# A block of 256 tokens for the first two slots, and router and remainder work on POOL

## The chip, the cores and the metric

The kernel is one program on one core of a Trainium2 chip. A core has TensorE (PE: matmuls and transposes, with its weight loads as PEld), VectorE (DVE), ScalarE (ACT), GpSimd (POOL) and SyncE (SP, which issues most of the DMA transfers); each works through a queue of its own, and semaphores order the queues against each other. The metric is the time of one execution on the device, in microseconds; less is better.

## The reference, cut to what matters

Three stages follow each other: a retention attention, a dense mixture of experts whose gate is normalised over rows and columns, and a second mixture in which each token goes to one expert. The change lies in the third and in the end of the second.

```python
def _moe2_ref(x, w_gate, w1, w2):            # x: 2304 tokens x 512, 8 experts, hidden size 1024
    logits = x @ w_gate
    expert_idx = np.argmax(logits, axis=1)
    logits_shift = logits - logits.max(-1, keepdims=True)
    probs = np.exp(logits_shift)
    probs /= probs.sum(-1, keepdims=True) + 1e-09
    gate_w = probs[np.arange(N), expert_idx]
    for e in range(E):
        mask = expert_idx == e
        if not mask.any():
            continue
        xe = x[mask]
        h = np.maximum(xe @ w1[e], 0.0)
        out[mask] = gate_w[mask, None] * (h @ w2[e])
```

All is float32. The kernel keeps the precision by splitting each operand into a high part (`hi`, the rounded value) and a remainder (`lo`, what the rounding left), and a product is hi·hi + hi·lo + lo·hi, three matmuls.

## The kernel before

The router finds each token's expert while the dense stage still runs. Tokens of one expert are put into slots of 128 lanes; at least 18 and at most 26 slots hold the 2304 tokens, and 22 are used with these inputs. The first 18 (`NFULL`) are written straight, the others stand behind branches. The router works in two halves: the first half of the tokens (`NEARLY` blocks of 128), whose dense result is done early, gets its ranks during the dense stage, and slots 0 and 1 are filled from it alone; the second half follows once the last dense blocks are done.

The steps of the router (class `Router`) are: `logit_parts` (logits of a block, tile `rpl`, then `L`), `choose` (maximum and one-hot `oh`), `count` (two matmuls `prk` over the one-hots), `totals`, `slots`, `experts` (the list `eidx` of each slot's expert and `echg`, whether the slot's weights differ from those before), `ranks`, `lanes` (the one-hot `Bm` of each token's lane, one operation for each block of 128 tokens), `slots_of`, `onehot` (`r_Z`), `rows` (18 matmuls `pz`, then the token list `gidx` and the scatter list `sidx`), and `gates` with `row_gates` (the gate values of the tokens by an accurate exponential, carried to the slots' rows by 18 matmuls `pzg`). Many of them call DVE through an object `Pumped`, whose line 408 is the line of all operations sent through it: after each it also issues the next operation of a background list, here the gate values.

The third stage is the class `Top1`. For a slot, `gather` fetches its 128 tokens (`xg`, an indirect DMA that POOL issues), `tx` transposes them (`ptx`, then `xth` on ACT and `xtl` on DVE), `load` fetches the expert's weights in eight transfers of 512 KB that SP issues (left out by the hardware condition `echg` where the expert stays), and `split` turns each of the eight pieces `raw` into a high part on ACT (`op0h` to `op6h` and `u7h`) and a remainder on DVE (`op0l` to `op6l`, `u7l`). Pieces 0 to 3 are the first weights, 4 to 7 the second. `hidden` multiplies (two halves of 12 matmuls 128x512, `phs`), `relu` writes `hrow`, `th` transposes it back (`pth`, then `hth` on ACT and the remainder `htl` on DVE) in two halves, and `result` does 24 matmuls 128x512 (`pys`): the first 8 use the high part of the first half of h, the next 4 its remainder, then the second half in the same way. `finish` scales by the gate on ACT and scatters the rows (POOL); `keep` stores an unscaled result in `o` until the gates exist.

While a slot runs, the pieces of the next are split. PE, DVE and ACT issue in the order in which the code is written (`MANUAL`); POOL and SP are ordered by a scheduler. Slots 0 and 1 stand out of line: their steps are written between those of the router, in the last block of the listing.

The remainder is the helper of line 40, one DVE operation with two inputs:

```python
def split_lo(eng, out, src, hi):
    return eng.tensor_tensor(out=out, in0=src, in1=hi.bitcast(F32), op=ALU.subtract)
```

Of the kernel before, what the change touches and what calls it, by code (L numbers as in the profile page):

```python
# [783 lines left out]
class Router:  # L784
# [50 lines left out]
    def choose(self, b, pool):  # L835
# [82 lines left out]
    def gates(self, b, pool):  # L918
# [6 lines left out]
        d = pool.tile([128, n, E], F32, name=f"gd{b}")  # L925
        g = pool.tile([128, n], F32, name=f"g{b}")
# [137 lines left out]
    def experts(self, pool):  # L1064
        v, res = self.v, self.res

        def T(shape, nm):
# [3 lines left out]
        end, cmp, cn = T([E], "end"), T([NSLOT, E], "cmp"), T([NSLOT], "cn")  # L1071
        es, z, ei1 = T([NSLOT], "es"), T([NSLOT], "z"), T([1], "ei1")
        v.tensor_tensor(out=end, in0=self.sta, in1=self.ns, op=ALU.add)
        v.tensor_tensor(
            out=cmp, in0=end.unsqueeze(1).to_broadcast([128, NSLOT, E]),
            in1=t.unsqueeze(2).to_broadcast([128, NSLOT, E]), op=ALU.is_le,
        )
        v.tensor_reduce(out=cn, in_=cmp, axis=AX.X, op=ALU.add)
        v.tensor_scalar(out=cn, in0=cn, scalar1=-1.0, scalar2=None, op0=ALU.add)
        v.scalar_tensor_tensor(  # L1080
            out=es, in0=cn, scalar=self.ei[:, 0:1], in1=cn, op0=ALU.is_ge, op1=ALU.add
        )
        v.tensor_scalar(out=ei1, in0=self.ei, scalar1=1.0, scalar2=None, op0=ALU.add)
        v.tensor_scalar(
            out=z, in0=cn, scalar1=0.0, scalar2=ei1[:, 0:1], op0=ALU.is_lt, op1=ALU.mult
        )
        v.tensor_tensor(out=es, in0=es, in1=z, op=ALU.add)
        v.tensor_scalar(out=es, in0=es, scalar1=float(E - 1), scalar2=None, op0=ALU.min)
        v.tensor_copy(res["eidx"], es)
        v.tensor_tensor(  # L1090
            out=z[:, 1:], in0=es[:, 1:], in1=es[:, 0:NSLOT - 1], op=ALU.not_equal
        )
# [20 lines left out]
    def rows(self, pool):  # L1113
# [43 lines left out]
class Top1:  # L1157
# [194 lines left out]
def build(ctx, tc, q, k, v, moe_w_gate, moe_w1, moe_w2, moe2_w_gate, moe2_w1, moe2_w2,  # L1352
# [136 lines left out]
    with tc.manual_schedule(engines=order):  # L1489
# [65 lines left out]
        }  # L1555
        for n, u in enumerate(range(2 * E - 1, -1, -1)):
# [150 lines left out]
```

## Time and profile before

| | us |
|---|---|
| median of 3 runs | 1976.94 |
| lowest and highest | 1976.7, 1980.82 |
| the profiled execution | 1978.74 |
| its span in the trace | 1977.0 |
| PE busy in the span | 1950.3 |
| DVE busy | 1256.2 |
| ACT busy | 868.3 |
| POOL busy | 180.8 |

The span runs from the first to the last instruction that the trace holds; the execution's own time is 1.7 us longer. The attention ends after some 230 us, the dense stage fills most of the rest, slot 0 begins near 1686 us in the trace and each slot behind the first ones takes about 12 us. A DVE or POOL operation is recorded from its start to its end, and a matmul's record is longer than the distance to the next one, since matmuls are pipelined: for these, the distance is the cost. Under "idle before" stands how long the engine had been idle and what ended that.

### The profile page before, as it was taken

To read this page: it belongs to the slowest core of one execution; us is meant where nothing else is said; L and a number is where in the kernel's file an instruction comes from. 1 tells how busy PE (TensorE), PEld (TensorE's weight loads), DVE (VectorE), ACT (ScalarE), POOL (GpSimd) and SP (SyncE) were. 2 spreads that over 40 slices of the span, in tenths; PEclk is the share of its full clock that TensorE was granted. 3 is DMA by queue.
4 is the path that set the end of the run, shared out by engine and by line. 5 is a ranking of instruction groups with operands and counts; after the bars stand their busy time and mean duration, and the time that the engine had idled before them with its cause. 6 is when DMAs were issued, how large, how long until landed. Compare 5 with 4: busy or idle time off the path is not lost.

```text
span 1977.0 us, 25401 instructions
## 1 busy us (share of the span) xinstructions
PE 1950.3 (99%) x9608; PEld 1626.9 (82%) x9608; DVE 1256.2 (64%) x2089; ACT 868.3 (44%) x1484; POOL 180.8 (9%) x200
## 2 busy tenths in 40 slices
PE   8999999999999999999999999999999999999998
PEld 7877888888888888888888888888888888778886
DVE  7997565555555555555565555665556665889998
ACT  6765424322223333233334333333333334489997
POOL 6662000000000000000010000000000000122211
PEclk9999999999999999999999999999999999999999
DMA  5531111111111011111211211111111213111755
GB/s 130 140 69 65 43 43 43 43 43 43 43 43 36 29 43 43 43 43 43 95 51 43 64 43 43 63 44 43 64 43 43 64 45 126 37 50 44 281 192 220
DMA packets 112111, 134.94 MB, mean 68 GB/s; under 512 B 62190, under 2 KB 62446, under 8 KB 111600
## 3 DMA queue, kind: packets, MB, share of 16 engines
q1 hardware_dynamic: 106960, 121.92, 19.3%
q0 software_dynamic: 3680, 11.02, 1.7%
q8 instruction: 77, 1.26, 0.3%
q10 hardware_dynamic: 1344, 0.33, 0.1%
q14 instruction: 50, 0.41, 0.1%
HBM read 182.53 MB, written 12.58 MB: 99 GB/s over the span
## 4 chain that ended last, share of the span: by engine, by line
PE 77%; issue 9%; DVE 8%; DMA 2%; POOL 2%; ACT 1%; SPq 0%; POOLq 0%; DVEq 0%; ACTq 0%
PE pyt L731 39%; PE pha L609 17%; PE phc L609 9%; PE phr L706 5%; PE phb L609 4%; DMA out_dram<-o,sidx 2%; DVE qbd L40 1%; POOL xg L1186 1%; DVE s L40 1%; POOL out_dram L1344 1%; DVE xa L287 1%; PE rpl L832 1%; DVE Sf L249 1%; DVE vlo L33 1%; DVE kT L33 1%
## 5 line engine op out<-in xcount | busy, mean ns | idle before, releaser
L731 PE MATMUL pyt<-w2hi,hhi 128*128 128x512 f32 x1024 | 402.2, 393 | 0.6 <-DVE xa L742 0.6
L731 PE MATMUL pyt<-w2hi,hlo 128*128 128x512 f32 x1024 | 398.9, 390 | 0.0
L731 PE MATMUL pyt<-w2lo,hhi 128*128 128x512 f32 x1024 | 398.5, 389 | 0.0
L635 ACT ACTIVATE q<-pha 128x512 f32<-128x512 f32 x192 | 114.6, 597 | 271.4 <-PE pha L609 268.9
L623 ACT ACTIVATE hhi<-q 128x512 fp32r<-128x512 f32 x192 | 121.4, 632 | 248.6 <-DVE q L631 248.6
L731 PEld LDWEIGHTS pyt<-w2hi,hlo 128*128 128x128 f32 x1024 | 192.2, 188 | 40.6
L731 PEld LDWEIGHTS pyt<-w2hi,hhi 128*128 128x128 f32 x1024 | 192.3, 188 | 40.3 <-DVE xa L742 1.4
L731 PEld LDWEIGHTS pyt<-w2lo,hhi 128*128 128x128 f32 x1024 | 192.4, 188 | 38.9
L624 DVE SCALAR_TENSOR_TENSOR hlo<-q,hhi 128x512 fp32r<-128x512 f32 x192 | 133.0, 692 | 96.8 <-ACT hhi L623 90.8
L742 DVE SCALAR_TENSOR_TENSOR xa<-pyt,P,xa 128x512 f32<-128x512 f32 x140 | 105.0, 750 | 134.5 <-PE pyt L731 133.7
L631 DVE TENSOR_TENSOR q<-phb,q 128x512 f32<-128x512 f32 x64 | 44.3, 692 | 166.6 <-PE phb L609 166.6
L742 DVE SCALAR_TENSOR_TENSOR xb<-pyt,P,xb 128x512 f32<-128x512 f32 x120 | 90.0, 750 | 90.4 <-PE pyt L731 90.3
L631 DVE TENSOR_TENSOR q<-phc,q 128x512 f32<-128x512 f32 x128 | 87.7, 685 | 34.0 <-PE phc L609 33.1
L561 ACT ACTIVATE w3h<-raw 128x512 fp32r<-128x512 f32 x31 | 19.6, 631 | 159.0 <-DVE raw L567 158.9
L567 DVE TENSOR_TENSOR raw<-raw 128x512 f32<-128x512 f32 x124 | 85.1, 686 | 1.1
L40 DVE TENSOR_TENSOR w2lo<-raw,w2hi 128x512 fp32r<-128x512 f32 x124 | 84.6, 683 | 0.0
L714 DVE SCALAR_TENSOR_TENSOR rlo<-phr,rhi 128x512 fp32r<-128x512 f32 x32 | 22.1, 691 | 87.7 <-ACT rhi L713 87.7
L587 ACT ACTIVATE w2hi<-raw 128x512 fp32r<-128x512 f32 x124 | 77.1, 622 | 0.0
L561 ACT ACTIVATE w4h<-raw 128x512 fp32r<-128x512 f32 x31 | 19.6, 631 | 115.2 <-DVE raw L567 115.2
L40 POOL TENSOR_TENSOR op2l<-xb,op2h 128x1024 fp32r<-128x1024 f32 x1 | 2.4, 2389 | 713.1 <-ACT op2h L494 713.1
L224 POOL TENSOR_SCALAR_AFFINE_SELECT s<-s 128x512 fp32r<-128x512 f32 (+1 forms) x96 | 57.3, 635 | 49.8 <-DVE s L40 49.8
L1186 POOL DMA_INDIRECT xg<-x2d,gidx x24 | 38.1, 1587 | 217.3 <-PE phc L609 100.6
(392 smaller groups left out, 4634.7 us busy)
## 6 DMA issues: line engine op xcount, KB each, us to landing
raw<-in_moe_w_dram SPq DMA_DIRECT2D x180, 512.0 KB
raw<-in_moe_w_dram SPq DMA_DIRECT2D x62, 1024.0 KB
kt<-in_k_dram SPq DMA_DIRECT2D x32, 128.0 KB
vt<-in_v_dram SPq DMA_DIRECT2D x32, 128.0 KB
qt<-in_q_dram SPq DMA_DIRECT2D x32, 128.0 KB
x2d<-xa SPq DMA_DIRECT2D x10, 256.0 KB
xbd<-xb SPq DMA_DIRECT2D x1, 2048.0 KB
xb<-xbd SPq DMA_DIRECT2D x2, 1024.0 KB
```

What stands on the lines that cost most here:

```text
L40: return eng.tensor_tensor(out=out, in0=src, in1=hi.bitcast(F32), op=ALU.subtract)
L567: nc.vector.tensor_tensor(out=q(*out), in0=q(*a), in1=q(*b), op=op)
L587: nc.scalar.activation(hi, self.raw2[:, fc, :], AF.Copy)
L609: self.nc.tensor.matmul(bank, ww[:, k, 128 * p:128 * p + 128], xx[:, k, :], start=start and n == 0, stop=stop and n == 5, skip_group_check ...
L623: nc.scalar.activation(hi, c, AF.Relu)
L624: nc.vector.scalar_tensor_tensor(out=lo, in0=c, scalar=0.0, in1=hi.bitcast(F32), op0=ALU.max, op1=ALU.subtract)
L631: self.nc.vector.tensor_tensor(out=s, in0=p, in1=s, op=ALU.add)
L635: self.nc.scalar.activation(t, c, AF.Copy)
L706: nc.tensor.matmul(pt[:, j, :], w[:, k, 128 * j:128 * j + 128], xr[x][:, xi, k, :], start=n == 0, stop=n == 11,)
L731: nc.tensor.matmul(pt, hh, ww, start=n == 0, stop=n == 11)
L742: nc.vector.scalar_tensor_tensor(out=acc, in0=pt, scalar=P[:, i, e:e + 1], in1=acc, op0=ALU.mult, op1=ALU.add)
L1186: self.nc.gpsimd.indirect_dma_start(out=self.xg[t % 3], out_offset=None, in_=self.x2d[0:rows, :], in_offset=bass.IndirectOffsetOnAxis(ap=i ...
```

## The change

Slots 0 and 1 become one block of 256 tokens. `block_hidden` multiplies with the weights as the stationary operand and both slots' tokens as the moving one, in four quarters of 24 matmuls 128x256 (`phb`), so that h comes out transposed already: its high part (`hb`) is written by ACT and its remainder by DVE, and the transposes `pth` of these slots are gone. The results of the two slots are still 24 matmuls each. For that, both slots' gathers go to the place where slot 0's was, and both `tx` into the last dense unit.

The router's `experts` is rewritten for POOL, where a reduction is a tree of additions and fused operations are split into two; every second `Bm` of the second half goes to POOL; `rows` issues the gathers of slots 2 and 3 right after `gidx`. The remainders of u7 (slot 0), op4 (slot 2), then inside slot 2 of u7, op1, op3 and op5, and inside slot 3 of op1 and op4, go to POOL. The gate values of the first half are issued in the last dense units, in steps between the products; those of the second half inside slot 2, four operations behind each split. Three slots' results are kept unscaled (tiles `o`, now four) and finished in slot 3 instead of two finished in slot 2.

```diff
-            (nc.gpsimd if i % 4 == 3 and b == 0 else v).tensor_scalar(
+            (nc.gpsimd if (i % 2 if b else i % 4 == 3) else v).tensor_scalar(
...
     def experts(self, pool):
-        v, res = self.v, self.res
+        g, res = self.nc.gpsimd, self.res
...
+        g.tensor_tensor(out=end, in0=self.sta, in1=self.ns, op=ALU.add)
+        g.tensor_tensor(
+            out=cmp, in0=t.unsqueeze(2).to_broadcast([128, NSLOT, E]),
+            in1=end.unsqueeze(1).to_broadcast([128, NSLOT, E]), op=ALU.subtract,
+        )
+        g.tensor_scalar(out=cmp, in0=cmp, scalar1=0.0, scalar2=None, op0=ALU.is_ge)
+        for h in (4, 2):
+            g.tensor_tensor(out=cmp[:, :, 0:h], in0=cmp[:, :, 0:h], in1=cmp[:, :, h:2 * h], op=ALU.add)
...
+        g.tensor_tensor(out=cn, in0=cmp[:, :, 0:1], in1=cmp[:, :, 1:2], op=ALU.add)
...
         v.tensor_copy(res["gidx"], tok)
+        then()
...
-    def split(self, c):
+    def split(self, c, pool=False):
         hi, lo = self.unit(c)
         self.nc.scalar.activation(hi, self.raws[c], AF.Copy)
-        split_lo(self.nc.vector, lo, self.raws[c], hi)
+        split_lo(self.nc.gpsimd if pool else self.nc.vector, lo, self.raws[c], hi)
...
+    def block_hidden(self, g, mid=None):
+        ph = self.php.tile([128, 2, 256], F32, name="phb2", tag="ph")
+        for j in range(2):
+            if j and mid:
+                mid()
+            f0 = 256 * g + 128 * j
+            n = 0
+            for k in range(KD):
+                wh, wl = self.unit(k)
+                for w, x in ((wh, 0), (wl, 0), (wh, 1)):
+                    self.nc.tensor.matmul(
+                        ph[:, j, :].rearrange("p (s t) -> p s t", s=2), w[:, f0:f0 + 128],
+                        self.xts[x][:, :, k, :], start=n == 0, stop=n == 11,
+                    )
+                    n += 1
+        hi, lo = (t[:, 2 * g:2 * g + 2, :] for t in self.hb)
+        self.nc.scalar.activation(hi, ph, AF.Relu)
+        self.nc.vector.scalar_tensor_tensor(
+            out=lo, in0=ph, scalar=0.0, in1=hi.bitcast(F32), op0=ALU.max, op1=ALU.subtract
+        )
+    def block(self, s):
+        return tuple(t[:, :, 128 * s:128 * s + 128] for t in self.hb)
...
-    def slot(self, t, mid=None):
+    def slot(self, t, mid=None, pooled=(), tick=lambda: None, kept=False):
+        def split(c):
+            self.split(c, c in pooled)
+            tick()
 
...
-        self.finish(t, py)
+            split(4)
+            split(5)
+        o = self.keep(t, py) if kept else self.finish(t, py)
...
+        gates0 = Pumped(nc.vector)
...
-            D.hidden(u)
+            if n == NEARLY + 4:
+                gates0.bg.append(ro.gates(0))
+            D.hidden(u, (), lambda: gates0.step(2))
...
+                gates0.step(1 if j < 6 else 8)
...
-                t1.gather(0)
+                for t in range(2):
+                    t1.gather(t)
...
+                    if j in (5, 6):
+                        t1.tx(j - 5, aux, "rt")
                     if j < 7:
                         t1.split(j)
-                    if j == 5:
-                        t1.tx(0, aux, "rt")
...
-        t1.gather(1)
-        t1.split(7)
-        ro.v.bg = [ro.gates(0, tmp)]
-        h0, h1 = t1.begin(), t1.begin()
-
-        ph = t1.hidden(0, 0, None, range(0, 2))
-        next(lp)
-        ph = t1.hidden(0, 0, ph, range(2, 4))
+        t1.block_hidden(0, lambda: next(lp))
         drain(lp)
-        t1.relu(0, ph, h0[0])
+        t1.split(7, True)
         ro.choose(1, tmp)
-        ro.v.bg.append(ro.gates(1, tmp))
-        ph = t1.hidden(0, 1, None, range(0, 1))
+        t1.block_hidden(1)
         ro.count(1)
-        t1.hidden(0, 1, ph, range(1, 4))
-        t1.relu(1, ph, h0[0])
         ro.totals(1)
         ro.slots(tmp)
-        t1.th(0, *h0)
-        t1.th(1, *h0)
-        t1.tx(1, t1.ptp, "pt")
-        py = t1.result(*h0[1:])
         ro.experts(tmp)
         t1.ahead(2)
         for c in range(4, 8):
             t1.load(2, c)
-        o0 = t1.keep(0, py)
-
         ro.ranks(1)
+        t1.block_hidden(2)
         ro.lanes(1)
         ro.slots_of(tmp)
-        ph = t1.hidden(1, 0)
-        t1.relu(0, ph, h1[0])
-        ph = t1.hidden(1, 1)
-        t1.relu(1, ph, h1[0])
+        t1.block_hidden(3)
         ro.onehot(tmp)
-        ro.rows(tmp)
-        for t in (2, 3):
-            t1.gather(t)
-        t1.th(0, *h1)
-        t1.th(1, *h1)
+        py = t1.result(*t1.block(0))
+        o0 = t1.keep(0, py)
+        py = t1.php.tile([128, DM], F32, name="pys1", tag="ph")
+        t1.result(*t1.block(1), py, slice(0, 8))
+        ro.rows(tmp, lambda: [t1.gather(t) for t in (2, 3)])
         for c in range(4):
             t1.split(c)
-        py = t1.result(*h1[1:], None, slice(0, 12))
-        t1.split(4)
+        t1.result(*t1.block(1), py, slice(8, 24))
         t1.tx(2, t1.ptp, "pt")
-        t1.result(*h1[1:], py, slice(12, 24))
+        t1.split(4, True)
         t1.split(5)
-        ro.v.rest()
         t1.ahead(3)
         o1 = t1.keep(1, py)
+        bg = Pumped(nc.vector)
+        bg.bg = [ro.gates(1, tmp)]
+        o2 = t1.slot(2, None, (7, 1, 3, 5), lambda: bg.step(4), True)
+        bg.rest()
         rg = ro.row_gates(tmp)
         next(rg)
 
         def mid():
             drain(rg)
-            t1.finish(0, o0, o0)
-            t1.finish(1, o1, o1)
-
-        for t in range(2, NFULL):
-            t1.slot(t, mid if t == 2 else None)
+            for t, o in enumerate((o0, o1, o2)):
+                t1.finish(t, o, o)
+        for t in range(3, NFULL):
+            t1.slot(t, mid if t == 3 else None, (1, 4) if t == 3 else ())
```

On DVE, at the turn to slot 2: before, from the products `r_Z` of the router's one-hots on. `op6l` and `u7l` are remainders of slot 2's own weights, `op0l` and those behind it of slot 3's, `htl` is the remainder of h.

```order
L408 TENSOR_TENSOR r_Z<-r_Z,gparts 128x18x26 x3
L40 TENSOR_TENSOR op6l<-raw_13843,op6h 128x1024
L40 TENSOR_TENSOR u7l<-raw_13844,u7h 128x1024
L40 TENSOR_TENSOR op0l<-raw_101,op0h 128x1024
L40 TENSOR_TENSOR htl<-pth,hth 128x512
L40 TENSOR_TENSOR op1l<-raw_101,op1h 128x1024
L40 TENSOR_TENSOR op2l<-raw_102,op2h 128x1024
L40 TENSOR_TENSOR xtl<-ptx,xth 128x512
L40 TENSOR_TENSOR htl<-pth,hth 128x512
```

The same place now, from the `xtl` of slot 2 to the first `htl`; `gd` and the tiles `g_` are gate values.

```order
L40 TENSOR_TENSOR xtl<-ptx,xth 128x512
L40 TENSOR_TENSOR op5l<-raw_13867,op5h 128x1024
L40 TENSOR_TENSOR op6l<-raw_13868,op6h 128x1024
L946 TENSOR_TENSOR gd_14553<-L_8949,m_14206 128x64
L348 TENSOR_SCALAR g_msk<-gd_14553 128x64
L350 TENSOR_SCALAR g_xc<-gd_14553 128x64
...
L360 TENSOR_SCALAR g_ki<-g_k 128x64
L40 TENSOR_TENSOR op0l<-raw_101,op0h 128x1024
L363 TENSOR_SCALAR g_q<-g_r 128x64
L366 SCALAR_TENSOR_TENSOR g_q<-g_q,g_r 128x64 x3
L40 TENSOR_TENSOR htl<-pth,hth 128x512
```

The products `r_Z` and the remainder of u7 are no longer ahead of the first `htl`; twelve operations of the gate values are, four of them left out above.

On POOL, behind the gathers of slots 0 and 1: before, only gathers and scatters follow.

```order
L913 TENSOR_SCALAR Bm<-c_8941,ro_13022 128x128 x2
L1186 DMA xg_13847<-x2d,gidx_69 128x512
L1186 DMA xg_14104<-x2d,gidx_69 128x512
L1186 DMA xg_14105<-x2d,gidx 128x512
L1186 DMA xg_13847<-x2d,gidx 128x512
```

Now, from the end of the expert list on.

```order
L1121 CAST echg<-r_z 128x25
L1212 DMA xg_14140<-x2d,gidx 128x512
L1212 DMA xg_13872<-x2d,gidx 128x512
L1212 DMA xg_13873<-x2d,gidx 128x512
L1212 DMA xg_14140<-x2d,gidx 128x512
L40 TENSOR_TENSOR op4l<-raw_13866,op4h 128x1024
L40 TENSOR_TENSOR u7l<-raw_13869,u7h 128x1024
L40 TENSOR_TENSOR op1l<-raw_101,op1h 128x1024
L1212 DMA xg_13872<-x2d,gidx 128x512
L40 TENSOR_TENSOR op3l<-raw_102,op3h 128x1024
L40 TENSOR_TENSOR op5l<-raw_13867,op5h 128x1024
```

Ahead of these stand 20 operations of the list with four `Bm` between them, and ahead of those the remainder of u7 for slot 0; all three came from DVE.

## Rows read from the trace of the kernel before

**Rows 1.** The page's first part: busy us of each engine, share of the span, instructions.

```profile
PE 1950.3 (99%) x9608; PEld 1626.9 (82%) x9608; DVE 1256.2 (64%) x2089; ACT 868.3 (44%) x1484; POOL 180.8 (9%) x200
```

**Rows 2.** Windows of slots 2, 3 and 4; columns in the prediction.

```profile
1720.06:1733.49 13.43, 13.30 (x80) 10.80 (x78) 11.49 (x17) 10.05 (x14) 2.79 (x3) 1.00 0.17 51
...
1733.49:1747.20 13.71, 12.60 (x62) 10.03 (x61) 13.06 (x13) 13.04 (x17) 4.71 (x4) 1.00 0.23 78
...
1747.20:1759.55 12.35, 12.35 (x62) 10.12 (x60) 11.21 (x12) 11.15 (x14) 3.01 (x2) 1.00 0.14 43
```

**Rows 3.** Waits of PE from 1677 us on: sum, count, mean.

```profile
PE pth L1265 <- ACT hrow L1258: 1.1, 1, 1.1
...
PE pz L1118 <- DVE r_Z L408: 1.1, 1, 1.1
...
PE prk L859 <- DVE g_k L354: 1.0, 1, 1.0
...
PE ptx L1232 <- DMA xg<-x2d,gidx: 0.9, 1, 0.9
...
PE ptx L1232 <- ACT L L833: 0.3, 1, 0.3
...
PE pys L1283 <- ACT hth L1267: 0.2, 1, 0.2
```

**Rows 4.** Windows behind the wait for g_k; the granted clock stands third from the end.

```profile
1694.00:1696.00 2.00, 2.00 (x7) 1.58 (x6) 2.00 (x17) 0.00 (x0) 0.00 (x0) 0.56 0.00 0
...
1696.00:1698.00 2.00, 2.00 (x8) 1.38 (x7) 1.66 (x13) 0.61 (x2) 0.00 (x0) 0.59 0.00 0
```

**Rows 5.** Timeline of PE, the first of 24 matmuls 128x256 and what follows them.

```profile
237.25 0.28 PE L706 MATMUL phr<-xrh,w0h 128*128 128x256 f32 x1
...
240.12 0.40 PE L609 MATMUL phc<-op3h,w3h 128*128 128x512 f32 x1
```

**Rows 6.** Timeline of PE: 24 hidden matmuls apart, and four transposes.

```profile
1704.35 0.39 PE L1253 MATMUL phs<-op0h,xth 128*128 128x512 f32 x1
...
1709.56 0.39 PE L1253 MATMUL phs<-op3h,xtl 128*128 128x512 f32 x1
...
1751.28 0.60 PE L1265 MATMUL pth<-ident,hrow 128*128 128x128 f32 x4
...
1751.63 0.48 PE L1253 MATMUL phs<-op2h,xth 128*128 128x512 f32 x1
```

**Rows 7.** Timeline of POOL and DVE in the dense stage.

```profile
987.55 2.39 POOL L40 TENSOR_TENSOR op2l<-xb,op2h 128x1024 fp32r<-128x1024 f32 x1 [713.07 <-ACT op2h L494]
...
988.23 0.75 DVE L742 SCALAR_TENSOR_TENSOR xa<-pyt,P,xa 128x512 f32<-128x512 f32 x1 [1.97 <-PE pyt L731]
...
988.90 2.13 DVE L40 TENSOR_TENSOR op0l<-xb,op0h 128x1024 fp32r<-128x1024 f32 x1
...
1002.27 1.21 DVE L40 TENSOR_TENSOR op5l<-xb,op5h 128x1024 fp32r<-128x1024 f32 x1
```

**Rows 8.** Timeline around slot 1's end, several engines.

```profile
1691.77 0.18 ACT L833 ACTIVATE L<-rpl 128x8 f32<-128x8 f32 x1 [1.53 <-PE rpl L832]
...
1712.35 0.18 DVE L408 CAST gidx<-r_tok 128x26 uint32<-128x26 f32 x1
...
1713.45 0.99 POOL L1186 DMA_INDIRECT xg<-x2d,gidx  x1 [55.57 <-ACT hth L1267]
...
1716.85 0.63 PE L1232 MATMUL ptx<-ident,xg 128*128 128x128 f32 x4 [0.87 <-DMA xg<-x2d,gidx]
...
1720.81 0.50 PE L1253 MATMUL phs<-op0h,xtl 128*128 128x512 f32 x1
```

**Rows 9.** Timeline and groups: Bm on both engines, a 512-column remainder on POOL.

```profile
1553.45 1.22 POOL L913 TENSOR_SCALAR Bm<-c,ro 128x128 bf16<-128x128 bf16 x2 [545.27 <-PE pyt L731]
...
1554.03 0.70 DVE L408 TENSOR_SCALAR Bm<-c,ro 128x128 bf16<-128x128 bf16 x3
...
L40 POOL TENSOR_TENSOR klo<-kt,khi 128x512 fp32r<-128x512 f32 x16 | 20.6, 1290 | 9.5 <-DMA gq_sb<-in_c_gq_dram 7.9 <-POOL s L224 1.2 <-ACT khi L149 0.4
```

More of the change, by code (lines that the diff above doesn't have):

```diff
@@ L383, in drain, with __init__, tile @@
             return s.value
+class Slab:
+    def __init__(self, ap):
+        self.ap, self.off, self.tags = ap, 0, {}
+    def tile(self, shape, dt, name, tag):
+        n = shape[1]
+        if tag not in self.tags:
+            self.tags[tag] = self.ap[:, self.off:self.off + n]
+            self.off += n
+        t = self.tags[tag]
+        return t if dt == F32 else t.bitcast(dt)
 class Pumped:
@@ L916, in lanes, with gates @@
             )
-    def gates(self, b, pool):
+    def gates(self, b, pool=None):
         nc, v, r = self.nc, self.nc.vector, self.B[b]
         i0, n = r["i0"], r["n"]
-        d = pool.tile([128, n, E], F32, name=f"gd{b}")
-        g = pool.tile([128, n], F32, name=f"g{b}")
+        if pool is None:
+            d, g = r["eq"], r["mm"]
+            pool = Slab(self.xt.rearrange("p a b -> p (a b)"))
+        else:
+            d = pool.tile([128, n, E], F32, name=f"gd{b}")
+            g = pool.tile([128, n], F32, name=f"g{b}")
         v.tensor_tensor(
@@ L1070, in experts @@
         t = self.c("t")
-        end, cmp, cn = T([E], "end"), T([NSLOT, E], "cmp"), T([NSLOT], "cn")
+        end, cmp, cn = T([E], "end"), T([NSLOT, E], "cmp"), T([NSLOT, 1], "cn")
         es, z, ei1 = T([NSLOT], "es"), T([NSLOT], "z"), T([1], "ei1")
[L1073 to L1076, printed above, removed]
-        )
@@ L1078, in experts @@
[L1078 to L1084, printed above, removed]
+        g.tensor_tensor(out=end, in0=self.sta, in1=self.ns, op=ALU.add)
+        g.tensor_tensor(
+            out=cmp, in0=t.unsqueeze(2).to_broadcast([128, NSLOT, E]),
+            in1=end.unsqueeze(1).to_broadcast([128, NSLOT, E]), op=ALU.subtract,
+        )
@@ new lines, in experts @@
+        g.tensor_scalar(out=cmp, in0=cmp, scalar1=0.0, scalar2=None, op0=ALU.is_ge)
+        for h in (4, 2):
+            g.tensor_tensor(out=cmp[:, :, 0:h], in0=cmp[:, :, 0:h], in1=cmp[:, :, h:2 * h], op=ALU.add)
+        g.tensor_tensor(out=cn, in0=cmp[:, :, 0:1], in1=cmp[:, :, 1:2], op=ALU.add)
+        cn = cn.rearrange("p s a -> p (s a)")
+        g.tensor_scalar(out=cn, in0=cn, scalar1=-1.0, scalar2=None, op0=ALU.add)
+        g.tensor_scalar(out=es, in0=cn, scalar1=self.ei[:, 0:1], scalar2=None, op0=ALU.is_ge)
@@ L1085, in experts @@
+        g.tensor_tensor(out=es, in0=es, in1=cn, op=ALU.add)
+        g.tensor_scalar(out=ei1, in0=self.ei, scalar1=1.0, scalar2=None, op0=ALU.add)
+        g.tensor_scalar(
             out=z, in0=cn, scalar1=0.0, scalar2=ei1[:, 0:1], op0=ALU.is_lt, op1=ALU.mult
         )
[L1087 to L1091, printed above, removed]
-        )
@@ L1094, in experts @@
-        v.scalar_tensor_tensor(
-            out=res["echg"][:, 1:], in0=t[:, 1:], scalar=self.inc[:, E - 1:E], in1=z[:, 1:],
-            op0=ALU.is_lt, op1=ALU.mult,
-        )
-        v.tensor_copy(res["nslot"], self.inc[:, E - 1:E])
+        g.tensor_tensor(out=es, in0=es, in1=z, op=ALU.add)
+        g.tensor_scalar(out=es, in0=es, scalar1=float(E - 1), scalar2=None, op0=ALU.min)
+        g.tensor_copy(res["eidx"], es)
+        g.tensor_tensor(out=z[:, 1:], in0=es[:, 1:], in1=es[:, 0:NSLOT - 1], op=ALU.subtract)
@@ L1100, in onehot @@
+        g.tensor_scalar(
+            out=z[:, 1:], in0=z[:, 1:], scalar1=0.0, scalar2=0.5, op0=ALU.is_equal, op1=ALU.is_lt
+        )
+        g.tensor_scalar(
+            out=cn, in0=t, scalar1=self.inc[:, E - 1:E], scalar2=None, op0=ALU.is_lt
+        )
+        g.tensor_tensor(out=z[:, 1:], in0=z[:, 1:], in1=cn[:, 1:], op=ALU.mult)
+        g.tensor_copy(res["echg"][:, 1:], z[:, 1:])
+        g.tensor_copy(res["nslot"], self.inc[:, E - 1:E])
     def onehot(self, pool):
@@ L1111, in onehot, with rows @@
         v.tensor_tensor(out=Z[:, :, 2, :], in0=A1, in1=bc(self.c("i")), op=ALU.mult)
-    def rows(self, pool):
+    def rows(self, pool, then):
         nc, v, res, Z = self.nc, self.v, self.res, self.Z
@@ L1168, in __init__ @@
         self.xts = [pool.tile([128, 2, KD, 128], F32R, name=f"xt{x}") for x in "hl"]
-        self.xg = [pool.tile([128, DM], F32, name="xg0")]
+        self.xg = [pool.tile([128, DM], F32, name=f"xg{i}") for i in range(2)]
         self.regs = {}
@@ L1308, in slot @@
         if nxt:
-            self.split(1)
+            split(1)
         self.relu(1, ph, h)
         if nxt:
-            self.split(2)
+            split(2)
             self.tx(t + 1, self.ptp, "pt")
```

17 lines of the change are left out of this document (9 added, 8 removed).

## The prediction

> **What bounds the kernel now.** I read the busy line first: TensorE (PE) works 1950.3 us of a span of 1977.0 [rows 1], so time can come only from where PE idles, runs slowly or does work that can go. The windows of slots 2, 3 and 4 come next [rows 2]; their columns after the sum are PE, PEld, DVE, ACT, POOL, granted clock, DMA share and GB/s. In slot 4 PE is busy all 12.35 us, and so it is in the slots behind it; slot 2 takes 13.43 and slot 3 takes 13.71. The slots of one stream follow each other on PE, so whatever moves the start of slot 5 moves the end by as much. Then the waits of PE over the last 300 us [rows 3]: hrow (ScalarE, ACT) 1.1, r_Z 1.1, g_k 1.0, the gather xg 0.9, and 0.2 to 0.3 each for L and hth. All lie before 1721 us but part of the first, which stands for one instruction in slot 3. A third view shows a loss that is no wait: between 1694 and 1698 the granted clock is 0.56 and 0.59 [rows 4], that is 1.2 GHz for most of it, right after PE's wait for g_k; I put the loss at 1.9 us (4 us at 0.575 do the work of 2.3, which loses 1.7; the fall begins and ends a little outside).
>
> **The change part by part.** I walked the engines' queues of the changed program in order with the durations of the rows, and compare the start of the third hidden matmul of slot 2 (1720.81 before [rows 8]), of slot 3 (1733.49 [rows 2]) and of slot 5 (1759.55).
>
> *The block.* The 72 matmuls of 256 columns that follow the router's last logits cost 2.87/24 = 0.1197 each [rows 5], 8.62 us; they replace 36 of 512 columns at 5.21/23 = 0.2267 (the 24 from the first to the second of [rows 6]), 8.16 us: +0.5. Four transposes cost 1751.63 - 1751.28 = 0.35 [rows 6]. Sixteen pth transposes go, and four ptx move ahead of the logits: 5 x 0.35 = -1.8. The waits for hrow and r_Z and the small ones for L and hth go: 1.1 + 1.1 + 0.3 + 0.2 = -2.7. The wait for g_k (VectorE, DVE) stays about 1.1: the ranks need oh, and oh stands behind u7's remainder. Before, that remainder was in DVE's queue; now it is on POOL, starts after u7h, which starts after the last L (1691.77 [rows 8]) and takes 1.05 of ACT, and runs to about 1695.9, while the block's second quarter covers PE to 1694.9 only. I take the 1.9 of the low clock as gone, since the matmuls around it are shorter and the wait is as long; if it stays, the result is 1.9 higher. New are three waits in front of slot 2. gidx comes at 1710.7 instead of 1712.5; from there to ptx took 4.3 [rows 8], and 16 result matmuls (3.6) follow it on PE, so ptx waits 1.5 instead of 0.9. Then xth: 1.1. Then xtl: 1.5, for it stands in DVE behind op0l to op3l (4 x 1.14), and op0 must land first, which the router's list now on POOL decides (end about 1709.7, plus a load that I estimate at 2.0 from the 2.4 between the end of the gather's issue and ptx [rows 8]). Together 0.5 - 1.8 - 2.7 - 1.9 + 0.6 + 1.1 + 1.5 + 0.1 = -2.6, and 0.2 to 0.3 comes back in the last dense unit, where ptx of slot 1 now stands: **-2.4** at the third hidden matmul.
>
> *Slot 2.* This is what decides. POOL gets the remainders of op4, u7, op1, op3 and op5, DVE the second half's gate values, four operations behind each remainder. What POOL costs is shown in the dense stage [rows 7]: op2l on POOL takes 2.39, from 987.55 to 989.94. DVE's op0l beside it was due at 988.90 and is recorded with 2.13, which is the 1.04 until POOL ended and then its own 1.09; undisturbed such an operation takes 1.21. In the same stretch xa, which reads PSUM, runs in its usual 0.75 beside POOL's op2l. A second pair 10 us later shows the same. So a DVE operation with both inputs in SBUF stands still while POOL's runs. In slot 2 the queue of DVE from xtl to the remainder htl of the first half of h is op5l, op6l, 12 gate operations, op0l: 3 x 1.14 = 3.4, the gate operations 0.2 each as the small row of gidx [rows 8], 2.5, and htl 0.6. Into it fall four POOL operations, op4l, u7l, op1l and op3l, 4 x 2.39 = 9.6, of which 0.7 is past when it begins: 15.4 in all. PE in that time has 22 hidden matmuls, 8 transposes of th and tx, 8 result matmuls and four transposes more, 30 x 0.227 + 3 x 0.35 = 7.9, and then the ninth result matmul wants htl: a wait of 7.3. The second half's htl comes 1.3 late in the same way (op5l on POOL). Without waits slot 2 from its third matmul is 11.9; with them 20.3, against 12.7 before: **+7.7**.
>
> *Slots 3 and 4.* The row gates (three products over 18x26, the sums, the gate itself) and three scalings of o, which cost slots 2 and 3 together 1.1 + 1.4 us above slot 4 before [rows 2], now fall into slot 3 alone, and op1l and op4l on POOL hold DVE for another 4.8. DVE's slack is what a slot leaves it, 12.35 - 11.21 = 1.1 [rows 2], in each. I get 29.2 instead of 26.1 for the two: **+3.2**. (The POOL work takes two remainders, 2.3, from DVE in exchange; that is in the sum.)
>
> *What costs nothing.* The first half's gate values run beside the last dense matmuls, where DVE is 64% busy over the span [rows 1]; two o more are kept by ACT, which has slack (11.15 of 12.35 with its waits [rows 2]). If this cover were gone, 33 operations of 0.2 would cost up to 6.6, but nothing on PE waits for them there. The gather of slot 1 goes to the dense stage with slot 0's (0.99 of POOL [rows 8], which is 9% busy over the span); three scatters of o go a slot later, and only o's buffers, now four, wait for them. One bound is wide: POOL's some 20 small operations for the expert list are not in the trace before. Its nearest rows are Bm at 0.61 [rows 9] and the 512-column remainder at 1.29, against 2.39 for 1024: 0.19 plus 2.15 ns per column. By that line the list ends as above. If each costs 0.1 to 0.2 more, op0 lands 2 to 4 us later and PE waits 2.3 to 4.5 more; if the list were free, at most the 1.5 of xtl would go.
>
> The Bm rows [rows 9] are weak evidence on another point: three DVE Bm, each with one SBUF input, take 0.70 in all while POOL does two at 0.61, so they are not held whole. The Trainium skill (SBUF — State Buffer, section Who interferes with whom) says that an operation with two SBUF inputs contends with GpSimd's reads, that copies, casts and tensor_scalar can take the shared ports as well, and that the loser of the pair is blocked for the whole instruction. By the row the single-input gate operations run free, and the sum is +8.5; by the rule in full they would be held too, and it would be +9.6.
>
> **The sum** is -2.4 + 7.7 + 3.2 = +8.5 against the profiled execution (1978.74 us), 1987.2 there. That execution stands 1.8 above the median, 1976.94, so on the median I forecast 1985.5.
>
> **The rivals.**
> *A, the slots don't feel POOL.* If DVE and POOL run side by side in the slots, the walk gives -2.4 for the block, slot 2 is near even, and DVE has gained seven remainders: together -4.4, or 1972.5. For it: the 0.70 of the three Bm; nothing stops DVE between two POOL operations. Against it: the pair of [rows 7] and the one behind it, which are the same operation at the same size.
> *B, near even.* The holding is as shown but POOL falls behind: its remainders start later than I let them, when DVE has passed htl, so that two of the four fall behind htl, and htl of the second half is not late: 8.5 - 2 x 2.39 - 1.3 = +2.4, or 1979.3. For it: POOL's queue holds the list, four gathers and the remainders, in one row. Against it: a late remainder delays the matmul that wants it.
> *C, slower still.* The list on POOL sets the start of slot 2 (0.2 per operation more, +4.5), or the wait of 7 us for htl is followed by the low clock as the one before 1694 was [rows 4]: 16 result matmuls at 0.2 more, +3.2. Together 1988.7 to 1993. It decides from the point where op0 lands after 1714.
>
> **How the numbers follow.** The forecast has 0.56 with a range of its own of 1981.5 to 1988.7, from the bounds above (a load's landing at 1 or 3 us is 1 either way, a POOL remainder of 2.0 instead of 2.39 takes 1.6 off, the low clock 1.9 on). A has 0.18, B 0.13, C 0.13. The range of 8 in 10 runs from 1972.5 to 1992: it takes in B, most of C and A down to its own time. About 0.2%, 4 us, is what a measurement of this kernel tells from no change. A lies at that bound and gives 0.12 to faster and 0.06 to no change, B 0.12 to no change and 0.01 to slower: faster 0.12, no change 0.18, slower 0.70.
>
> **What would show it.** Right: in the profile after, DVE's op5l, op6l and op0l in slot 2 are recorded with 2.5 to 3.6 us instead of 1.2, PE waits some 7 us for htl of the first half in slot 2, and slot 3 is over 14 us; the waits for hrow and r_Z are gone, and slot 2 begins 2 to 3 us earlier. Wrong: remainders of 1.2 on DVE beside POOL's 2.39, or PE's first long wait on op0h (then it is the list), or POOL's remainders behind the matmul that wants them.

## The result

The changed kernel takes 1988.97 us (median of 4 runs, 1988.01 to 1992.45) against 1977.38 (4 runs, 1976.7 to 1980.82): a ratio of 1.0059, 95% interval 1.0046 to 1.0071, so 11.6 us slower. The forecast was 1985.5, in a range of 1972.5 to 1992; its own narrower range, 1981.5 to 1988.7, ends 0.3 below the measured time.

The profiled execution took 1992.45 us with a span of 1990.7, 13.7 more than the span of before. Of that, 3.5 us lie in the attention, which the change doesn't touch: the first matmul of [rows 5] stands at 240.73 instead of 237.25. In two of the experiments below, whose attention is the same too, it stands at 236.47 and at 240.53, so I compare stretches and not positions.

| stretch on PE | before | forecast | after |
|---|---|---|---|
| first matmul of [rows 5] to the last logits | 1453.5 | +0.3 | 1454.3 (+0.8) |
| last logits to the third hidden matmul of slot 2 | 30.0 | -2.7 | 25.6 (-4.4) |
| from there to slot 3 | 12.7 | +7.7 | 23.6 (+10.9) |
| slots 3 and 4 | 26.1 | +3.2 | 28.6 (+2.5) |
| sum | | +8.5 | +9.8 |

Behind slot 5 nothing differs: from its start to the last matmul are 209.5 and 209.6. The +0.8 of the first row is not told from scatter: up to the last logits the experiments on the changed kernel have the same code, and their traces show 1453.4 to 1454.7 there.

The remaining 1.8 between 9.8 and the 11.6 of the medians is not in this table; the profiled execution of before stood 1.4 above its own median. The last experiment shows a likely place. Its program is that of before up to slot 2 (but for one more buffer for o), and from the last logits to the third hidden matmul of slot 2 its trace has 28.9 instead of 30.0: there PE's clock doesn't fall behind the wait for g_k. So the 30.0, and the -4.4 worked out from it, hold 1.1 that this stretch does not always cost, and against that trace the block is worth 3.3. That the median run of before also lacks the low clock is not shown.

The first part of the page after (busy us, share, instructions), to be held against [rows 1], and the windows of slots 2, 3 and 4, which answer to [rows 2]:

```profile
PE 1953.9 (98%) x9640; PEld 1631.1 (82%) x9640; DVE 1264.5 (64%) x2064; ACT 866.9 (44%) x1481; POOL 210.5 (11%) x232
```

```profile
1719.91:1744.26 24.35, 15.52 (x61) 11.82 (x62) 22.60 (x31) 12.55 (x16) 15.96 (x8) 0.79 0.13 36
1744.26:1757.29 13.03, 13.03 (x80) 10.88 (x78) 11.16 (x17) 9.44 (x13) 4.61 (x3) 1.00 0.08 21
1757.29:1772.84 15.55, 13.15 (x62) 9.87 (x61) 12.89 (x12) 14.24 (x19) 8.76 (x6) 1.00 0.21 74
```

PE does 3.6 us more and yet fills less of the span; slot 2 is the place, and slot 4 is now longer than slot 3. The waits of PE from 1670 us on in the changed kernel (sum, count, longest), to be held against [rows 3], whose third figure is the longest as well:

```profile
PE pys L1334 <- DVE htl L40: 9.1, 2, 8.8
PE pth L1316 <- ACT hrow L1309: 1.5, 1, 1.5
PE prk L874 <- DVE oh L423: 1.0, 1, 1.0
PE ptx L1258 <- DMA xg<-x2d,gidx: 0.9, 1, 0.9
PE phs L1279 <- ACT xth L1260: 0.7, 1, 0.7
PE phs L1279 <- DVE op3l L40: 0.6, 1, 0.6
```

The wait for r_Z is gone, prk still waits 1.0, and a new wait of 8.8 us for htl is longer than all of [rows 3] together. The wait for hrow is not one of the block: it stands in slot 4 now, and before it stood in slot 3, as PE's timeline of the kernel before has it:

```profile
1738.84 0.66 PE L1265 MATMUL pth<-ident,hrow 128*128 128x128 f32 x4 [1.11 <-ACT hrow L1258]
```

The timeline of DVE in slot 2 (start, us, operation) tells what htl stood behind:

```profile
1719.89 0.69 DVE L40 TENSOR_TENSOR xtl<-ptx,xth 128x512 fp32r<-128x512 f32 x1 [0.16 <-ACT xth L1260]
1721.78 6.01 DVE L40 TENSOR_TENSOR op5l<-raw,op5h 128x1024 fp32r<-128x1024 f32 x1 [1.20 <-ACT op5h L1247]
1727.71 3.40 DVE L40 TENSOR_TENSOR op6l<-raw,op6h 128x1024 fp32r<-128x1024 f32 x1
1731.04 0.21 DVE L946 TENSOR_TENSOR gd<-L,m 128x64 f32<-128x64 f32 x1
1731.28 0.20 DVE L348 TENSOR_SCALAR g_msk<-gd 128x64 f32<-128x64 f32 x1
1731.39 3.05 DVE L350 TENSOR_SCALAR g_xc<-gd 128x64 f32<-128x64 f32 x1
...
1737.46 0.68 DVE L40 TENSOR_TENSOR htl<-pth,hth 128x512 fp32r<-128x512 f32 x1
...
1741.49 0.68 DVE L40 TENSOR_TENSOR htl<-pth,hth 128x512 fp32r<-128x512 f32 x1
1742.09 1.90 DVE L964 CAST gparts<-g 128x8 bf16<-128x8 f32 x1
```

And the timeline of POOL in the same slot:

```profile
1721.93 2.42 POOL L40 TENSOR_TENSOR op4l<-raw,op4h 128x1024 fp32r<-128x1024 f32 x1
1724.30 2.40 POOL L40 TENSOR_TENSOR u7l<-raw,u7h 128x1024 fp32r<-128x1024 f32 x1
1727.07 2.96 POOL L40 TENSOR_TENSOR op1l<-raw,op1h 128x1024 fp32r<-128x1024 f32 x1 [0.38 <-ACT op1h L1247]
...
1732.03 2.35 POOL L40 TENSOR_TENSOR op3l<-raw,op3h 128x1024 fp32r<-128x1024 f32 x1
1741.59 2.38 POOL L40 TENSOR_TENSOR op5l<-raw,op5h 128x1024 fp32r<-128x1024 f32 x1 [7.21 <-ACT op5h L1247]
```

op5l is recorded with 6.01: POOL's op4l and u7l end at 1726.70, and op5l's own 1.09 follows [rows 7]. op6l ends 1.1 behind POOL's op1l (1730.03). g_xc, a TENSOR_SCALAR with one input in SBUF and 0.2 long elsewhere, ends at 1734.44, 0.06 behind op3l; its record begins 0.64 before that of op3l, and what held it in that time is not shown. A CAST takes 1.90 and ends with op5l of POOL. htl reads PSUM: the first one has no operation of POOL beside it, the second (1741.49) runs beside op5l and still takes its usual 0.68. PE, on its timeline, then runs on at half its speed:

```profile
1728.85 0.60 PE L1316 MATMUL pth<-ident,hrow 128*128 128x128 f32 x4
1738.20 1.22 PE L1334 MATMUL pys<-op4h,htl 128*128 128x512 f32 x2 [8.76 <-DVE htl L40]
...
1740.92 0.63 PE L1334 MATMUL pys<-op6h,hth 128*128 128x512 f32 x1
...
1743.06 0.43 PE L1334 MATMUL pys<-u7l,hth 128*128 128x512 f32 x1
...
1744.26 0.39 PE L1279 MATMUL phs<-op0h,xth 128*128 128x512 f32 x1
```

The window of the profile there (PE, PEld, DVE, ACT, POOL, granted clock, DMA share, GB/s) names the cause, 1.2 GHz:

```profile
1740.00:1742.00 2.00, 2.00 (x6) 1.54 (x5) 1.90 (x7) 1.51 (x2) 0.41 (x1) 0.50 0.00 0
...
1743.00:1745.00 2.00, 2.00 (x10) 1.58 (x9) 1.90 (x5) 0.55 (x2) 0.97 (x1) 0.97 0.04 8
```

The first 11 result matmuls behind the wait, 1738.20 to 1743.06, take 4.86 us where 11 at 0.2267 [rows 6] would take 2.49: 2.4 lost. The wait and these are 11.2, which is the 10.9 that slot 2 grew by, within 0.3.

### The profile page after: what moved, and what is told of

The parts are those of the page before. It is cut to its first block, busy times and chain, and to the rows that moved or that the text cites. A ratio compares the mean times of both kernels' runs of the same rounds, so it can differ in the third digit from the quotient of the medians.

```text
span 1990.7 us, 25472 instructions
## 1 busy us (share of the span) xinstructions
PE 1953.9 (98%) x9640; PEld 1631.1 (82%) x9640; DVE 1264.5 (64%) x2064; ACT 866.9 (44%) x1481; POOL 210.5 (11%) x232
## 4 chain that ended last, share of the span: by engine, by line
PE 78%; issue 9%; DVE 7%; DMA 2%; POOL 2%; ACT 1%; SPq 0%; POOLq 0%; ACTq 0%; DVEq 0%
PE pyt L746 39%; PE pha L624 17%; PE phc L624 9%; PE phr L721 5%; PE phb L624 4%; DMA out_dram<-o,sidx 2%; DVE qbd L40 1%; POOL xg L1212 1%; DVE s L40 1%; POOL out_dram L1400 1%; PE po L274 1%; DVE xa L287 1%; PE rpl L847 1%; PE pys L1334 1%; DVE Sf L249 1%
## 5 line engine op out<-in xcount | busy, mean ns | idle before, releaser
L576 ACT ACTIVATE w3h<-raw 128x512 fp32r<-128x512 f32 x31 | 19.6, 631 | 159.6 <-DVE raw L582 159.5
L576 ACT ACTIVATE w4h<-raw 128x512 fp32r<-128x512 f32 x31 | 19.6, 631 | 114.1 <-DVE raw L582 114.1
L928 POOL TENSOR_SCALAR Bm<-c,ro 128x128 bf16<-128x128 bf16 x6 | 4.0, 672 | 545.4 <-PE pyt L746 545.3
```

## The experiments

Each run states its median beside that of the kernel before, timed on the same chip. The last two columns are from one trace of each, in us. An interval behind a ratio is at 95%.

| kernel | us | before | third hidden matmul of slot 2 to slot 3 | slots 3 and 4 |
|---|---|---|---|---|
| before | | 1977.38 | 12.7 | 26.1 |
| changed | 1988.97 | 1977.38 | 23.6 | 28.6 |
| no remainders on POOL in slots 2, 3 | 1980.15 | 1977.26 | 15.2 | 29.0 |
| gate values between the router's operations | 1982.17 | 1977.26 | 17.3 | 28.4 |
| both of these | 1976.34 | 1977.26 | 12.3 | 27.5 |
| list on DVE | 1987.26 | 1977.26 | 21.3 | 28.9 |
| both, u7 on DVE | 1978.76 | 1977.61 | 13.5 | 27.5 |
| both, results finished one by one | 1974.61 | 1977.61 | 12.3 | 25.4 |
| all of these | 1973.46 | 1977.61 | 12.4 | 25.4 |
| POOL remainders in halves | 1988.53 | 1977.61 | 23.6 | 28.6 |
| before, results finished one by one | 1976.90 | 1978.47 | 12.7 | 24.7 |

**No remainders on POOL in the slots.**

```diff
-        t1.split(4, True)
+        t1.split(4)
-        o2 = t1.slot(2, None, (7, 1, 3, 5), lambda: bg.step(4), True)
+        o2 = t1.slot(2, None, (), lambda: bg.step(4), True)
-            t1.slot(t, mid if t == 3 else None, (1, 4) if t == 3 else ())
+            t1.slot(t, mid if t == 3 else None, ())
```

> Theory P (POOL's remainders in slots 2 and 3 hold DVE's operations): all seven remainders go back to DVE, the gate values stay in slot 2. DVE's queue ahead of the first htl of slot 2 is then 5 remainders of 1.14, 12 small ones of 0.21 and 0.6, 8.8 us, no longer than what PE has to do, so the wait of 8.8 us and the low clock behind it go; DVE still has some 17 us of work in slot 2 and gives 3 to 4 us of it to slots 3 and 4. About 1979 us (1975 to 1982). Theory G (the 33 gate operations put into slot 2 are what delays htl, POOL only relieves DVE): DVE gets 8 us more work ahead of and behind htl, so no faster than now, 1987 or more. Theory L (the expert list on POOL sets the start of slot 2): no change beyond 2 us, since the list stays.

1980.15 us, 8.8 less than the changed kernel, although DVE now does seven remainders more. Its operations in slot 2 are back to their own lengths; g_xc stands here for the single-input ones:

```profile
1722.06 1.22 DVE L40 TENSOR_TENSOR op5l<-raw,op5h 128x1024 fp32r<-128x1024 f32 x1
1723.30 1.23 DVE L40 TENSOR_TENSOR op6l<-raw,op6h 128x1024 fp32r<-128x1024 f32 x1
...
1724.81 0.19 DVE L350 TENSOR_SCALAR g_xc<-gd 128x64 f32<-128x64 f32 x1
...
1729.02 0.68 DVE L40 TENSOR_TENSOR htl<-pth,hth 128x512 fp32r<-128x512 f32 x1
```

The longest wait for htl is 2.2 instead of 8.8, and theory G falls: more work on DVE made it faster. L falls too, since the list stayed where it was. But P had the wait go altogether, and slots 3 and 4 still take 29.0.

**Gate values between the router's operations.**

```diff
         ro.choose(1, tmp)
+        ro.v.bg.append(ro.gates(1, tmp))
...
-        bg = Pumped(nc.vector)
-        bg.bg = [ro.gates(1, tmp)]
-        o2 = t1.slot(2, None, (7, 1, 3, 5), lambda: bg.step(4), True)
-        bg.rest()
+        ro.v.rest()
+        o2 = t1.slot(2, None, (7, 1, 3, 5), kept=True)
```

> The gate values of the second half are issued between the router's DVE operations, as before the change; POOL keeps its seven remainders. Theory P: DVE ahead of the first htl still has 3 remainders of 1.14 and stands behind three or four of POOL's 2.39, 11 to 13 us against PE's 8, so a wait of 3 to 5 us stays: about 1984 us (1981 to 1986). Theory G: the wait goes, slots 2 and 3 are no longer than before, and with the block's gain about 1974.

1982.17, where P expected 1981 to 1986. The longest wait for htl is 2.5, a little less than P's 3 to 5. POOL's remainders hold DVE as in the changed kernel, here DVE's remainders alone:

```profile
1721.56 2.83 DVE L40 TENSOR_TENSOR op5l<-raw,op5h 128x1024 fp32r<-128x1024 f32 x1 [1.15 <-ACT op5h L1247]
1724.32 3.42 DVE L40 TENSOR_TENSOR op6l<-raw,op6h 128x1024 fp32r<-128x1024 f32 x1
1727.66 3.40 DVE L40 TENSOR_TENSOR op0l<-raw,op0h 128x1024 fp32r<-128x1024 f32 x1
...
1731.58 3.88 DVE L40 TENSOR_TENSOR op2l<-raw,op2h 128x1024 fp32r<-128x1024 f32 x1
```

Taken one by one, the remainders are worth 8.8 and the gate values 6.8; they share a part, since either shortens the same queue.

**Both.** The two edits above together.

> Both at once: no remainder on POOL in slots 2 and 3, gate values of the second half between the router's operations. Theory P: slots 2 to 4 cost what they did before the change, and the block's gain stays (4.4 us in the traces up to the third hidden matmul of slot 2): about 1973 us (1971.5 to 1975). Theory G: the same as with the gate values moved alone, within 2 us of it. Theory L: 1976 or more.

1976.34, ratio 0.9993 (0.9984 to 1.0003): the slowdown is gone, 12.6 us below the changed kernel, and slot 2 costs 12.3. It is not the 1973 that P expected. Of the difference, 1.4 is in slots 3 and 4, 27.5 against 26.1; most of the rest is again what the stretches of the traces do not hold (here they add up to -2.6, and the medians differ by -0.9). ACT's timeline shows what slots 3 and 4 lose:

```profile
1741.42 0.60 ACT L1318 ACTIVATE hth<-pth 128x512 fp32r<-128x512 f32 x1 [0.66 <-PE pth L1316]
1743.91 1.95 ACT L1399 ACTIVATE o<-o,gate 128x512 f32<-128x512 f32 x3 [1.90 <-DVE gate L423]
1745.77 1.04 ACT L1247 ACTIVATE op3h<-raw 128x1024 fp32r<-128x1024 f32 x1
...
1751.07 0.58 ACT L1309 ACTIVATE hrow<-phs 128x512 f32<-128x512 f32 x1
```

ACT stands 1.90 for the gate, scales three tiles in 1.95, and is so late that PE waits 1.5 for hrow in slot 4.

**The list on DVE.** `experts` as it was before the change; all else as changed.

> The expert list alone goes back to DVE; everything else as changed. Theory L: op0's load starts earlier (the list took POOL from 1703.2 to 1712.9 us), slot 2 starts sooner, 3 to 4 us faster than the changed kernel: 1985. Theory P: within 1.5 us of the changed kernel (1989), since what follows the list in slot 2 is held by POOL anyway and PE's waits for xth and ptx there are 1.5 us together.

1987.26, 1.7 below the changed kernel, a little more than P allowed; the intervals of the two ratios overlap (1.0034 to 1.0068 and 1.0046 to 1.0071), so the times alone don't tell them apart. All four runs lie above L's 1985. In the trace two things offset each other: the wait for htl is 5.9 instead of 8.8, but that for the gather is 1.9 instead of 0.9, and with the 0.7 for xth behind it PE falls to the low clock (0.55 and 0.60 from 1716 to 1720), so that slot 2's third hidden matmul comes 26.9 behind the last logits instead of 25.6.

**u7 on DVE as well,** on top of both.

```diff
-        t1.split(7, True)
         ro.choose(1, tmp)
+        t1.split(7)
```

> Built on the run without remainders on POOL and with the gate values between the router's operations (1976.3 us). The remainder of slot 0's u7 goes back to DVE as well, behind oh instead of ahead of it. Theory P: the 2.42 us of oh beside that remainder becomes 0.2, PE's wait of 1.0 for oh goes, 1975.3 us. Rival: the wait was given back anyway, because the chain from oh to gidx sets ptx; then the ptx wait (0.75) grows by what oh's wait loses, since u7's remainder (1.2) now stands in DVE's chain: 1976.3.

1978.76, 2.4 above the run without it, and neither theory had that. The intervals overlap (0.9995 to 1.0013 and 0.9984 to 1.0003); the traces show the same difference, 2.5 from the last logits to slot 3. oh takes 0.45 instead of 2.42 and prk's wait is gone, as P says. But gidx comes 19.6 us behind the last logits, as without the edit (19.7), and ptx's wait grows to 2.2; the gather itself took 5.2 us from gidx to ptx instead of 3.8. All of that lies in POOL's issue of it, which begins 0.5 later behind gidx and takes 2.11 instead of 1.13; why is open. Loads of weights run beside both, at 131 GB/s here and 143 in the run without the edit. PE idles for most of 1714 to 1717, and then runs at the low clock; its windows:

```profile
1714.00:1716.00 2.00, 0.29 (x2) 0.00 (x0) 2.00 (x3) 0.73 (x1) 1.70 (x2) 1.00 0.43 131
1716.00:1718.00 2.00, 0.80 (x5) 0.56 (x6) 0.71 (x2) 0.79 (x2) 1.39 (x3) 1.00 0.47 121
1718.00:1720.00 2.00, 2.00 (x5) 1.32 (x6) 1.75 (x3) 2.00 (x3) 0.90 (x1) 0.58 0.67 182
1720.00:1722.00 2.00, 2.00 (x7) 1.56 (x6) 1.98 (x3) 2.00 (x3) 0.00 (x0) 0.56 0.26 90
```

So the rival was right that the chain to ptx decides. PE's waits ahead of slot 2 are 3.4 instead of 2.5, and 4 us at 0.57 lose another 1.7. That the idle time cost clock because it was now in one piece is argued from this trace; the run with the list on DVE is like it, and the run with all of these, which waits 1.9 for the gather and not for xth, keeps 1.00.

**Results finished one by one,** on top of both.

```diff
         def mid():
-            drain(rg)
-            for t, o in enumerate((o0, o1, o2)):
-                t1.finish(t, o, o)
+        def mid(t):
+            if t == 3:
+                drain(rg)
+            elif t < 7:
+                t1.finish(t - 4, kept[t - 4], kept[t - 4])
```

> Built on the same run (1976.3 us). The three kept results are scaled in slots 4, 5 and 6, one each, instead of all three in slot 3; the gate row is still made in slot 3. Theory A (ACT stands 1.9 us for the gate in slot 3 and scales three tiles in 1.95, which makes hrow of slot 4 late): slots 3 and 4 lose 1.5 to 2 us, 1974.6. Rival D (DVE's row gates are what lengthens slots 3 and 4): no change, 1976.3.

1974.61, ratio 0.9985 (0.9976 to 0.9994), as theory A says; that it is so to the tenth is luck, since the interval overlaps that of the run it is built on. What decides for A is the trace: slots 3 and 4 take 25.4, less than before the change, and the wait for hrow is gone.

**All of these.** Besides, the eight Bm of the second half on DVE, pz after 4 matmuls of slot 1's result, ptx ahead of its last 4.

> The two changes just named together, and besides all Bm on DVE, the 18 matmuls pz after 4 matmuls of slot 1's result instead of 8, and ptx of slot 2 ahead of its last 4. If the gains add: 1976.3 - 1.0 - 1.6 - 0.4 = 1973.3 us, 0.2% below the kernel before the change; if the chain to ptx sets the start of slot 2 whatever stands ahead of it, 1974.6.

1973.46, ratio 0.9983 (0.9974 to 0.9992): the fastest, 0.2% below the kernel before. From the version finished one by one its interval doesn't separate it, and so the 1973.3 of the added gains is not confirmed: from the last logits on, the stretches of its trace are within 0.1 of that version's, and the 0.8 by which it is shorter lies ahead of the last logits, where the programs are the same. The gather's wait is 1.9 here, so the chain to ptx still sets the start of slot 2.

**POOL remainders in halves,** in the changed kernel.

```diff
+        if pool:
+            for f in (slice(0, 512), slice(512, 1024)):
+                split_lo(self.nc.gpsimd, lo[:, f], self.raws[c][:, f], hi[:, f])
```

> The changed kernel with each POOL remainder issued as two operations of 512 columns (1.29 each by the rows of before) instead of one of 1024 (2.39). Theory P1 (an operation is held whole, and the two engines take turns): no operation of DVE is held more than 1.3, op5l in slot 2 falls from 6.0 to 2.4, the wait for htl falls from 8.8 to 5 or 6, 1985 to 1986 us. Theory P2 (POOL goes on with its next operation before DVE gets in, as the 6.0 of op5l suggests): op5l stays at 5 to 6 and the time at 1989 or above.

1988.53, no change. DVE's rows and then POOL's:

```profile
1720.19 6.26 DVE L40 TENSOR_TENSOR op5l<-raw,op5h 128x1024 fp32r<-128x1024 f32 x1 [0.34 <-ACT op5h L1247]
1726.37 2.31 DVE L40 TENSOR_TENSOR op6l<-raw,op6h 128x1024 fp32r<-128x1024 f32 x1
...
1730.32 3.23 DVE L352 TENSOR_SCALAR g_k<-g_xc 128x64 f32<-128x64 f32 x1
```

```profile
1720.30 2.56 POOL L40 TENSOR_TENSOR op4l<-raw,op4h 128x512 fp32r<-128x512 f32 x2
1722.80 2.55 POOL L40 TENSOR_TENSOR u7l<-raw,u7h 128x512 fp32r<-128x512 f32 x2
1725.94 3.86 POOL L40 TENSOR_TENSOR op1l<-raw,op1h 128x512 fp32r<-128x512 f32 x2 [0.59 <-ACT op1h L1247]
```

op5l is held through four operations of POOL, one behind the other, so shorter ones gave it no turn, as P2 says. At op1l they do take turns: its halves take 3.86 instead of 2.5, and op6l 2.31, one half and its own 1.1. The wait for htl stays at 8.7. What decides which engine gets its turn is left open.

**The kernel before, results finished one by one.**

> The kernel before the change, with nothing but its two kept results scaled in slots 3 and 4, one each, instead of both in slot 2 (three buffers for o instead of two). Theory A (ACT's wait for the gate and the scalings push hrow of the next slot): the wait of 1.1 for hrow in slot 3 and part of the 1.4 that slot 3 is longer than slot 4 go, 1 to 2 us: 1976. Then the block and the rest of the change without POOL's remainders are worth 1.5 us beside it (1974.6). Rival: the row gates on DVE fill the same time, no change, 1977.5.

1976.90 against 1978.47 beside it, ratio 0.9993 (0.9984 to 1.0002): the wait of 1.1 for hrow in slot 3 is gone (the 0.3 that its trace has for hrow is in slot 0), and slots 3 and 4 fall from 26.1 to 24.7, but the times alone don't tell it from no change. Against the kernel before, the version with the block stands at 0.9985; that the block and what of the change stays with it (the list, four Bm and slot 0's u7 on POOL, the order of gathers and gate values) are together worth about 1.6 us is a difference of two ratios whose intervals overlap.

The same trace bears on the low clock of [rows 4]. Up to slot 2 this is the program of before but for one more buffer for o, and PE waits for g_k as long; but in the windows from 1695 to 1705 the granted clock is 1.00, where [rows 4] have 0.56 and 0.59. The six matmuls between the last two rows below take 1.36 us, where the same six take 2.47 in the trace of before:

```profile
1696.58 0.20 PE L859 MATMUL prk<-oh,c 128*128 128x64 bf16 x1 [0.99 <-DVE g_k L354]
...
1697.20 0.39 PE L1253 MATMUL phs<-op1h,xtl 128*128 128x512 f32 x1
...
1698.56 0.39 PE L1253 MATMUL phs<-op3h,xtl 128*128 128x512 f32 x1
```

## Why the prediction was right, point by point

The direction and the mechanism were right. That the sum came as near as +8.5 to the +9.8 of the stretches is in part luck: slot 2 was taken 3.2 too small, the block 1.7 and slots 3 and 4 0.7 too dear. The measured time lies just above the forecast's own range and at the lower end of rival C's, and half of C came true.

*That POOL holds DVE in slot 2* was right and is shown: without those remainders the wait goes from 8.8 to 2.2, and op6l has the length that was forecast (3.40, in a forecast of 2.5 to 3.6). op5l does not (6.01, held by two remainders in a row), and op0l, which the forecast named too, ran free at 1.22; g_xc was held in its place. The sum is not touched by which operation is held, since all four remainders stood in it. The term was too small, 7.7 for 10.9, by other terms. DVE first waited 1.20 for op5h, which the working put at nothing, and was held some 10.0 us where it had 8.9; together the wait for htl was 8.8 and not 7.3. The second htl was waited for 0.3 and not 1.3. And rival C's second half came true: the low clock behind the wait took 2.4 us (3.2 were given for it), which the forecast had left out. The prediction's own figures also don't give its result: 15.4 - 7.9 is 7.5, and 11.9 + 7.5 + 1.3 is 20.7 and not 20.3.

*Single-input operations* were taken to run free, from the Bm rows [rows 9]. That choice was wrong for float32: g_xc 3.05 in the changed kernel and g_k 3.23 in the run with halves, 0.19 and 0.20 without POOL's remainders. The Trainium skill (SBUF — State Buffer, section Who interferes with whom) has casts and tensor_scalar among the operations that can contend with GpSimd, in modes that use both of DVE's ports. Here the trace agrees (3.05 and 1.90). The sum by that rule, +9.6, is nearer to +9.8, but how it follows is not worked out in the prediction, and with the errors above its nearness says little. The operations that read PSUM were right: the second htl kept its 0.68 beside op5l.

*The block* was right in direction and came out at -4.4 instead of -2.7, by errors that partly cancel. The terms for transposes and r_Z held, and prk's wait stayed at 1.0, as forecast. But 1.1 for hrow and 0.3 for L could not be won here: the wait for hrow stood in slot 3 (1738.84), and that for L stands ahead of the last logits, before and after. Too dear were the three waits in front of slot 2: ptx 0.9 for 1.5, xth 0.7 for 1.1, and xtl 0.2 for 1.5 (0.39 between the two matmuls around it instead of 0.2267). The last fell because the loads landed sooner: ACT starts op0h 1.1 us behind the end of the list (1713.96), where 2.0 was estimated from the gather. The low clock, -1.9, is gone in the trace (granted clock 1.00 from 1698 to 1702), but not shown to be gone by the block, as the prediction had it: the trace of the last experiment lacks it too, with the same wait for g_k and the matmuls of before. Against that trace the block is worth 3.3.

*Slots 3 and 4* came out at +2.5 for +3.2, but for other reasons. Their POOL remainders are worth 1.0 where the gate values are moved out of slot 2 (28.4 to 27.5), and nothing where they are not (28.6 to 29.0); finishing three results behind the gate in one slot is worth 2.1 (27.5 to 25.4). The prediction gave ACT slack for it and looked at DVE. The trace of before had the sign of it: ACT's late hrow in slot 3, which the prediction booked as a gain of the block.

*The list on POOL* stood in the sum as the 1.5 of xtl, with +2.3 to +4.5 if dearer; with the list on DVE the time is 1.7 lower, within the intervals.

## What to carry to other kernels

A remainder moved from a full DVE to an idle POOL is no relief where DVE's own operations read two inputs from SBUF: here POOL's 2.4 us stopped DVE for as long, to spare it 1.1. Look for one pair of such operations side by side in any trace of the same chip before moving work; it decided this case. And where a result must be scaled by something that comes late, spread the scalings over the stages that have room, since in one stage an engine with 10% of slack becomes the bound.

## What was not expected of the hardware

DVE's op5l was held through four operations of POOL in a row (6.26 us), and a float32 TENSOR_SCALAR of 64 columns with one input was recorded with 3.05 us beside POOL, about as long as a held remainder with two (3.40). Where u7 went back to DVE, a wait of 1.0 us went away and the trace still became 2.5 us longer up to slot 3: the gather came later, and PE ran at 1.2 GHz for 4 us behind the wait for it. And the same wait of 1.0 us for g_k, in the same program, was followed by 1.2 GHz in one trace (0.56 and 0.59) and by the full clock in another (1.00).
